# Attention and gated feed-forward on one core: another transfer model, another set of rules for the order

## Chip, cores and metric

The kernel runs on one core of one Trainium2 chip. The metric is the device time in microseconds (us); lower is better. Each engine of the core (TensorE or PE, ScalarE or ACT, VectorE or DVE, GpSimd or POOL, SyncE or SP) has its own instruction stream; semaphores tie them together. SP here issues all transfers (DMAs).

## The reference

One sequence of S = 2048 rows of width D = 512, in bf16. The result is the input plus an attention block plus a gated feed-forward block, both fed by the same layer norm. There are 32 heads of 16 elements each; the feed-forward is 1792 wide.

```python
def _A_ref(x, wqkv, wo):
    qkv = (x @ wqkv).reshape(B, S, 3, H, Dh).transpose(2, 0, 3, 1, 4)
    q, k, v = qkv[0], qkv[1], qkv[2]
    scores = jnp.einsum("bhqd,bhkd->bhqk", q, k) * (Dh ** -0.5)
    p = _softmax(scores, axis=-1)
    o = jnp.einsum("bhqk,bhkd->bhqd", p, v)
    return o.transpose(0, 2, 1, 3).reshape(B, S, D) @ wo

def _B_ref(x, w1, w3, w2):
    h = _silu(x @ w1) * (x @ w3)
    return h @ w2

x = A_x
xn = _layernorm(x, axis=-1)
return x + _A_ref(xn, A_wqkv, A_wo) + _B_ref(xn, B_w1, B_w3, B_w2)
```

## The kernel before

**Work.** Heads go four at a time (8 groups g), queries 512 at a time (4 chunks qc). A query unit u is one group with 256 queries; the first three units and the last sixteen are smaller, 128 queries for the most part. For each unit the scores are computed twice.

In pass one (p1) a row-tiled matmul of 32 contraction rows (L1371) writes scores of 128 queries against 512 keys into a bank of PSUM; two neighbouring banks hold 1024 scores, and VectorE takes the row maximum of each half (`tensor_reduce`, L1416). 998 of these run. In some places a "split" replaces part of this: ScalarE makes RB (L1484), and VectorE finishes it (L1409). The maxima of a unit are joined on GpSimd (L1538 to L1552, for the last units on VectorE at L1575), spread into Z (L1520, L1522), and brought as two extra rows into Q: by a DMA transpose (L1568) and two DMAs (L1564), or for the first and last units by matmuls (tile `AQ`). A DMA (L1502) also copies Q of each head into a block-diagonal tile BD.

In pass two (p2) the scores come again, transposed, keys on partitions, with the maximum already subtracted by the extra rows. The matmuls are row-tiled (L1653), or "wide" with BD as the moving operand over the full array. ScalarE takes the exponential of one bank of 512 (L1678), or of two neighbouring banks in one instruction of 1024 (L1709), a **pair**. Then PV (tile `PV`, L777) multiplies by V with a column of ones; ScalarE moves the result to U (L1773). The normaliser follows as a chain with one unit in it at a time: DMA Lc from U (L1794), reciprocal on GpSimd (L1798), DMA to DRAM rd (L1803), broadcast DMA back into R (L1807), multiply on GpSimd (L1834), and for odd groups four small DMAs (L1830).

The feed-forward (tiles `G`, `U`, with ScalarE at L1089, L1093, L1083 and GpSimd at L1060, L1064) and the output projection (`OUT`, at the end `OUTA` and `OUTB`) are fitted in between. Their weights come by DMA at L727 and L729, the residual at L1117, stores go at L1148.

**Order.** No instruction's place is written by hand. While the program is built, a planner keeps a clock for each engine and a ready time for each buffer, and gives out the next instruction to the engine that could start first. `pick_pe`, `pick_act`, `pick_dve`, `pick_pool` and `pick_sp` propose, each by cost figures in the code. For a transfer, `later_dma` notes `occ` (how long SP is taken by issuing it), `lat` (from issue to landing) and `busy` (the share of the transfer engines). The result is five static instruction lists. On the chip each runs strictly in its order, and only semaphores decide the times: a wrong cost figure gives waits, not wrong data.

**Rules.** The proposals depend on some 45 constants (`RULES`), among them `A_LEAD` (how long ahead a row maximum's scores are wanted), `PAIR_WAIT` (how long ScalarE may be held for a pair), `HEAT_FILL`, `HEAT_WIDE`, `HEAT_FORCE`. The planner cuts its progress into 256 segments of 12 steps; `TUNE` names for each segment one of the `SETS`, which override some constants.

**Heat.** `_heat` gives each matmul a weight, and `heat(t)` sums weight times duration over the 3.413 us before t. Below `HEAT_FILL` a filler matmul, whose result nobody reads (`fill_cand`), may be put in where it fits; below `HEAT_WIDE` pass two prefers its wide form; below `HEAT_FORCE` a matmul that works on columns is put in even if it doesn't fit ahead of the next score.

**Pairs.** `pick_act` looks at the first few waiting exponentials; if two lie in neighbouring banks and the second is ready no more than `PAIR_WAIT` later, they become one instruction.

Of the kernel before, what the change touches and what calls it, by code (L numbers as in the profile page):

```python
# [268 lines left out]
def _build(nc, A_x, A_wqkv, A_wo, B_w1, B_w3, B_w2, out):  # L269
# [48 lines left out]
    BD_END = 4  # L318
    NORM = "dddppppp"
# [12 lines left out]
        dict(PAIR_WAIT=0.15, RELAX=0.05),  # L332
        dict(P2_FRAG=0.0, URG_WAIT=0.05, A_LEAD=0.82, PAIR_WAIT=0.15),
        dict(P1_SLIP=0.15, P1_TRI=1, P2_MID=3, P1_EARLY=0.15),
        dict(P2_MID=3, PV_LEFT=2, TOL=0.15, PAIR_DEPTH=3),
        dict(LAZY_MAX=6.0, A_LEAD=0.55),
        dict(WIDE_LEAD=0.3, TOL=0.1),
        dict(A_LEAD=0.82, P2_MID=5, HEAT_WIDE=0.47),
        dict(TOL=0.0, PV_LEFT=2, A_LEAD=0.55, AGAIN=3),
        dict(RELAX=0.1, PACE=12000),  # L340
        dict(PAIR_TEN=0, TEN_MID=1),
        dict(A_LEAD=0.69, HEAT_FILL=0.82, URG_WAIT=0.15),
        dict(OUT_GATE=14, TOL=0.1),
        dict(PAIR_DEPTH=5, HEAT_TILE=0.5, PAIR_WAIT=0.15),
        dict(W_WAIT=0.1, RELAX=0.2),
        dict(HEAT_FORCE=0.5, PAIR_TEN=2),
        dict(P1_SLIP=0.15, BD_NEAR=0.5, RELAX=0.05, HEAT_TILE=0.5),
        dict(MIN_PIECE=3, LAZY_GAP=0.05, PAIR_TEN=0, HEAT_WIDE=0.57),
        dict(HEAT_FILL=0.82, PACE=3000, A_LEAD=0.82),
        dict(HEAT_FILL=0.82, PACE=12000, P1_SLIP=0.15, FILL_SLIP=0.1),  # L350
        dict(ROW_LEAD=0.55, WIDE_LEAD=0.45, BD_NEAR=0.1),
        dict(HEAT_FILL=0.7, LAZY_GAP=0.3, FILL_SLIP=0.1),
        dict(URG_WAIT=0.05, P1_EARLY=0.3, HEAT_WIDE=0.57, LAZY_MAX=1.0),
        dict(ROW_LEAD=0.62, FILL_SLIP=0.1),
        dict(BD_NEAR=0.5),
# [12 lines left out]
        dict(BD_NEAR=0.1),
        dict(P2_NEAR=0.1, HEAT_P1=0.35, A_LEAD=0.88, HEAT_WIDE=0.57),
        dict(HEAT_FILL=0.82),  # L370
        dict(FILL_SLIP=0.1, W_WAIT=0.1, P2_NEAR=0.02, WIDE_LEAD=1.0),
        dict(WIDE_LEAD=0.7, BD_NEAR=0.8, COUPLE=0.08, HEAT_P1=0.65),
        dict(A_LEAD=0.88, HEAT_WIDE=0.34, URG_WAIT=0.05),
        dict(WIDE_LEAD=0.7, BD_NEAR=0.1, W_WAIT=0.2),
        dict(A_LEAD=0.82),
        dict(PACE=12000, PAIR_WAIT=0.05, P2_NEAR=0.4, COUPLE=0.18),
        dict(HEAT_TILE=0.65, P2_MID=3, WIDE_LEAD=0.2, HEAT_FILL=0.82),
        dict(WIDE_LEAD=0.7, P2_NEAR=0.1, FILL_SLIP=0.0, A_LEAD=0.82),
        dict(PAIR_WAIT=0.1, HEAT_FILL=0.82),
        dict(TOL=0.05, BD_NEAR=0.1, AGAIN=2, PAIR_WAIT=0.0),  # L380
        dict(BD_NEAR=0.2),
        dict(HEAT_FILL=0.55, W_WAIT=0.2, HEAT_P1=0.65, MIN_PIECE=3),
        dict(RELAX=0.1, PAIR_DEPTH=2, FILL_SLIP=0.0, BD_NEAR=0.1),
        dict(A_LEAD=0.55, LAZY_MAX=1.0, COUPLE=0.25, P1_TRI=1),
        dict(HEAT_TILE=0.7, A_LEAD=0.72),
        dict(BD_NEAR=0.5, W_WAIT=0.2, PAIR_DEPTH=4, P1_SAME=0.2),
        dict(FILL_SLIP=0.2, WIDE_LEAD=0.3),
        dict(MIN_PIECE=2, TOL=0.05, WIDE_LEAD=0.7, W_WAIT=0.1),
        dict(A_LEAD=0.6, HEAT_FORCE=0.41, WIDE_LEAD=0.7),
        dict(A_LEAD=0.69, WIDE_LEAD=1.0),  # L390
        dict(HEAT_P1=0.55, BD_NEAR=0.5),
        dict(LAZY_GAP=0.3, A_LEAD=0.69),
        dict(A_LEAD=0.69, P1_EARLY=0.15, COUPLE=0.25),
        dict(PV_LEFT=3, MIN_PIECE=2, RELAX=0.05, P1_SLIP=0.15),
        dict(W_WAIT=0.1, ROW_LEAD=0.4),
        dict(COUPLE=0.04, OUT_GATE=20, HEAT_FILL=0.45, P1_SAME=0.05),
        dict(RELAX=0.05),
        dict(P1_EARLY=0.3, P1_SAME=0.05, HEAT_FILL=0.7, PAIR_TEN=0),
        dict(HEAT_FILL=0.45),
        dict(HEAT_P1=0.35, HEAT_FILL=0.45, PAIR_TEN=0),  # L400
        dict(PAIR_TEN=2, RELAX=0.05),
        dict(ROW_LEAD=0.55),
        dict(PACE=12000, MIN_PIECE=4, HEAT_P1=0.65, AGAIN=4),
        dict(PV_LEFT=8, HEAT_WIDE=0.57, TOL=0.05, LAZY_GAP=0.02),
        dict(HEAT_FILL=1.2, P2_FRAG=0.0, RELAX=0.2),
        dict(HEAT_FILL=0.5, WIDE_LEAD=1.0, HEAT_TILE=0.5, TOL=0.03),
        dict(ROW_LEAD=0.55, PV_LEFT=2, HEAT_FILL=0.7, PAIR_WAIT=0.0),
        dict(COUPLE=0.04, URG_WAIT=0.15, HEAT_WIDE=0.57),
        dict(HEAT_TILE=0.53),
        dict(A_LEAD=0.88, HEAT_WIDE=0.57, TOL=0.0),  # L410
        dict(LAZY_MAX=1.0, HEAT_FORCE=0.36, P2_MID=3),
        dict(PAIR_DEPTH=1, LAZY_MAX=6.0, A_LEAD=0.69, TRI_WAIT=0.1),
        dict(HEAT_FILL=0.55),
        dict(HEAT_FILL=0.5, BD_NEAR=0.5),
        dict(A_LEAD=0.69, HEAT_FORCE=0.42),
        dict(TRI_WAIT=0.3, P2_NEAR=0.0, P2_MID=2, BD_NEAR=0.8),
        dict(A_LEAD=0.6),
        dict(HEAT_P1=0.0, ROW_LEAD=0.43, AGAIN=4, LAZY_GAP=0.02),
        dict(P1_SAME=0.2, ROW_LEAD=0.43, P2_NEAR=0.4),
        dict(URG_WAIT=0.05, PAIR_WAIT=0.1, HEAT_WIDE=0.47),  # L420
        dict(LAZY_MAX=6.0, ROW_LEAD=0.62, P1_SLIP=-0.15),
        dict(MIN_PIECE=2, HEAT_FILL=0.4, RELAX=0.1, OUT_GATE=32),
        dict(COUPLE=0.18, P2_MID=2, HEAT_FILL=0.82),
        dict(P1_TRI=1, PACE=3000, P2_NEAR=0.2, PAIR_TEN=2),
        dict(HEAT_P1=0.0, HEAT_FILL=0.82),
        dict(PAIR_TEN=2, HEAT_FILL=1.2),
        dict(P1_SAME=-0.1, PACE=12000, HEAT_P1=0.55, TRI_WAIT=0.3),
        dict(A_LEAD=0.72),
        dict(HEAT_P1=0.49, PAIR_DEPTH=2, A_LEAD=0.69, HEAT_TILE=0.65),
        dict(HEAT_P1=0.61),  # L430
        dict(P1_SAME=0.2, A_LEAD=0.88),
        dict(ROW_LEAD=0.35, P2_FRAG=0.2, PAIR_DEPTH=5),
        dict(MIN_PIECE=2, ROW_LEAD=0.5),
        dict(PAIR_WAIT=0.05, W_WAIT=0.2),
        dict(BD_NEAR=0.2, TOL=0.03, WIDE_LEAD=0.3, P1_SLIP=0.15),
        dict(ROW_LEAD=0.4, P2_NEAR=0.2),
        dict(LAZY_MAX=6.0, HEAT_P1=0.65),
        dict(TOL=0.05),
        dict(ROW_LEAD=0.5),
# [24 lines left out]
    )
# [14 lines left out]
    class K:  # L479
# [15 lines left out]
        P1_SLIP=0.0,  # L495
# [55 lines left out]
    with ctx:  # L551
# [1793 lines left out]
```

## Time and profile before

| | us |
|---|---|
| median of 3 runs | 1198.87 |
| lowest, highest | 1196.85, 1200.25 |
| the profiled execution, its own time | 1193.87 |
| its span in the profile | 1192.1 |
| busy: PE, VectorE, ScalarE, GpSimd | 1123.6, 1166.7, 1166.2, 452.0 |
| first row maximum starts, last one ends | 14.25, 1168.4 |
| exponentials: of 512, of 1024 (pairs) | 1728, 160 |

The span runs from the first instruction to the last. Instructions of ScalarE overlap: one of 512 lasts 715 ns by its own record, and the next starts before it ends. So prices of ScalarE are read from start to start, and a busy time of 98% may hold small gaps. In a group of instructions the columns are: line, engine, operation, output<-input, count, then busy us and mean ns, then the idle time ahead of them and what ended it. Windows give for each stretch the busy us of each engine, the number of instructions that start in it, and the TensorE clock that was granted (1.00 is full speed).

### The profile page before, as it was taken

The numbers are of one execution on the slowest core, as the hardware profiler recorded it, in microseconds if no ns is written. First come the engines' busy times: TensorE is split into PE (matmuls) and PEld (weight loads), VectorE is DVE, ScalarE is ACT, GpSimd is POOL, SyncE is SP. The second block draws the span as 40 slices with busy tenths as digits, with TensorE's granted clock in tenths as the row PEclk, the third lists the DMA queues.
The fourth block names the chain that finished last, engine by engine and source line by source line (L and its number), as shares of the span: only waits on it lengthen the run. The fifth ranks groups of instructions, "written<-read, shape, count | busy, mean of one in ns | idle before, by whom it ended". The sixth has DMA issues, their size and how long they took to land.

```text
span 1192.1 us, 36419 instructions
## 1 busy us (share of the span) xinstructions
PE 1123.6 (94%) x15037; PEld 529.2 (44%) x15171; DVE 1166.7 (98%) x1091; ACT 1166.2 (98%) x2245; POOL 452.0 (38%) x888
## 2 busy tenths in 40 slices
PE   8989999999999999999999999999999999998998
PEld 4433434443444444334444444434434444354654
DVE  8999999999999999999999999999999999998995
ACT  8899999999999999999999999999999999998997
POOL 7145453444424254334432234533442214621220
PEclk9999999999999999999999999999999999999999
DMA  8233322211111121111111122111110112000010
GB/s 247 73 77 80 90 55 54 56 28 41 38 43 29 41 59 38 41 40 28 46 30 24 38 56 61 43 33 36 38 30 24 41 48 49 19 23 21 15 22 22
DMA packets 141641, 55.96 MB, mean 47 GB/s; under 512 B 103968, under 2 KB 141476, under 8 KB 141476
## 3 DMA queue, kind: packets, MB, share of 16 engines
q1 hardware_dynamic: 141476, 53.63, 17.4%
q8 instruction: 120, 1.97, 0.7%
q14 instruction: 45, 0.37, 0.1%
HBM read 38.93 MB, written 6.74 MB: 38 GB/s over the span
## 4 chain that ended last, share of the span: by engine, by line
ACT 67%; DVE 14%; PE 12%; DMA 3%; issue 2%; SPq 1%; POOL 1%
ACT PT L1678 51%; DVE part L1416 14%; ACT PT L1709 8%; PE ps L773 5%; PE ps L777 3%; PE ps L1371 2%; PE ps L1653 2%; ACT zg L1089 2%; ACT th L1083 1%; ACT ub L1093 1%; ACT U L1773 1%; DMA rd<-Rc 1%; ACT RB L1484 1%; DMA R<-rd 1%; ACT kq L961 1%
## 5 line engine op out<-in xcount | busy, mean ns | idle before, releaser
L1416 DVE TENSOR_REDUCE part<-ps 128x2 f32<-128x1024 f32 x998 | 1133.2, 1216 | 6.9 <-PE ps L1653 3.5
L1678 ACT ACTIVATE PT<-ps 128x512 bf16<-128x512 f32 x1728 | 918.8, 715 | 6.5 <-PE ps L1653 2.4
L1653 PE MATMUL ps<-QT,KT 32*128 32x256 bf16 (+1 forms) x3420 | 457.0, 258 | 8.8 <-DMA QT<-Zs 1.1
L1371 PE MATMUL ps<-KT,QT 32*128 32x512 bf16 x2158 | 431.5, 384 | 8.3 <-DVE part L1416 4.2
L1653 PEld LDWEIGHTS ps<-QT,KT 32*128 32x128 bf16 x3420 | 161.5, 93 | 167.1 <-ACT PT L1678 70.2
L777 PE MATMUL ps<-PT,Vaug 128*17 128x256 bf16 (+1 forms) x4672 | 197.9, 261 | 3.5 <-ACT PT L1678 0.7
L1709 ACT ACTIVATE PT<-ps 128x1024 bf16<-128x1024 f32 x160 | 177.0, 1123 | 0.3 <-PE ps L1653 0.2
L1371 PEld LDWEIGHTS ps<-KT,QT 32*128 32x128 bf16 x2158 | 107.9, 91 | 145.0 <-DVE part L1416 63.0
L773 PE MATMUL ps<-xnT,w 128*128 128x512 bf16 (+3 forms) x612 | 153.3, 309 | 12.4 <-ACT PT L1678 3.4
L1798 POOL TENSOR_TENSOR Rc<-Lc,mone 128x8 f32<-128x8 f32 (+1 forms) x69 | 104.8, 1519 | 117.3 <-DMA Lc<-U 116.9
L773 PE MATMUL ps<-BD,KT 128*128 128x256 bf16 (+1 forms) x790 | 135.1, 265 | 3.1 <-ACT PT L1709 0.9
L777 PEld LDWEIGHTS ps<-PT,Vaug 128*17 128x17 bf16 x4672 | 92.8, 90 | 75.6 <-issue 54.1
L773 PE MATMUL ps<-xnT,ident 128*128 128x512 bf16 (+3 forms) x314 | 80.5, 323 | 10.0 <-DVE part L1416 3.1
L773 PEld LDWEIGHTS ps<-xnT,w 128*128 128x128 bf16 x661 | 51.2, 97 | 82.6 <-issue 44.8
L777 PE MATMUL ps<-BD,KT 128*32 128x256 bf16 (+1 forms) x1848 | 83.5, 265 | 2.9 <-DMA BD<-QT 2.6
L773 PE MATMUL ps<-w,hT 128*128 128x128 bf16 (+3 forms) x335 | 81.7, 301 | 3.6 <-ACT U L1773 2.7
L1545 POOL TENSOR_TENSOR mx<-part 128x16 f32<-128x16 f32 (+1 forms) x60 | 14.2, 237 | 180.7 <-DVE part L1416 180.5
L1834 POOL TENSOR_TENSOR wk_on<-U,R 128x256 bf16<-128x256 f32 (+1 forms) x36 | 22.9, 635 | 139.6 <-DMA R<-rd 139.6
L773 PEld LDWEIGHTS ps<-BD,KT 128*128 128x128 bf16 x790 | 60.9, 98 | 32.5 <-ACT PT L1678 7.2
L1064 POOL TENSOR_TENSOR hT<-a,t 128x512 bf16<-128x512 f32 x56 | 71.0, 1268 | 2.4
L1834 POOL TENSOR_TENSOR on_b<-U,R 128x256 bf16<-128x256 f32 (+1 forms) x33 | 23.5, 711 | 126.1 <-DMA R<-rd 126.1
L1060 POOL TENSOR_SCALAR t<-th 128x512 f32<-128x512 bf16 x56 | 34.8, 621 | 84.4 <-ACT th L1083 82.8
(114 smaller groups left out, 753.8 us busy)
## 6 DMA issues: line engine op xcount, KB each, us to landing
w<-in_B_w_dram SPq DMA_DIRECT2D x112, 128.0 KB
R<-rd SPq DMA_DIRECT2D x55, 128.0 KB
QT<-qd SPq DMA_DIRECT2D x31, 128.0 KB
KT<-kd SPq DMA_DIRECT2D x28, 128.0 KB
BD<-QT SPq DMA_DIRECT2D x220, 10.5 KB
xr<-in_A_x_dram SPq DMA_DIRECT2D x16, 128.0 KB
out_dram<-osb SPq DMA_DIRECT2D x16, 128.0 KB
qd<-kq SPq DMA_DIRECT2D x15, 128.0 KB
```

The source lines that it names most:

```text
L773: return e.matmul(bank(bk)[:, c0 + a:c0 + b], make_lhsT(0, 128), rhs_ap(0)[:, a:b], start=start, stop=stop, **kw)
L777: ins = e.matmul(bank(bk)[32 * i:32 * i + m, c0 + a:c0 + b], make_lhsT(i), rhs if (a, b) == (0, ncols) else rhs[:, a:b], start=start, stop ...
L1060: q.append(_Item(lambda e: e.tensor_scalar(t1[:, :], th[:, ss, :], 1.0, 1.0, ALU.mult, ALU.add), [("th", ss)], [("t1",)], 0.62, 0.72))
L1064: q.append(_Item(lambda e: e.tensor_tensor(hT[:, hslot(idx), :], a32[:, :], t1[:, :], ALU.mult), [("a32",), ("t1",)], [("hT", hslot(idx))] ...
L1089: return [_Item(lambda e: e.activation(zg[:, ss, :], bank(bk), ACTF.Identity, scale=0.5), [("ps", bk)], [("zg", ss)], _c_act(512), cb=zg_d ...
L1371: ins = e.matmul(bank(held[i]), QT[32 * j:32 * j + 32, qs, q * 128:(q + 1) * 128], KT[32 * j:32 * j + 32, g, c_ * 512:(c_ + 1) * 512], sta ...
L1416: redq.append(_Item(lambda e: e.tensor_reduce(dst, banks, AX.X, ALU.max), writes, [("part", par, i_) for i_ in ix[:m]], _c_dve(512 * m), c ...
L1653: ins = e.matmul(bank(b)[:, i * nq:(i + 1) * nq], KT[32 * j:32 * j + 32, g, (k0 + i) * 128:(k0 + i + 1) * 128], QT[32 * j:32 * j + 32, qs, ...
L1678: expq.append(_Item(lambda e: e.activation(PT[:, sl, :], bank(b), ACTF.Exp, scale=SCALE), [("ps", b)], [("PT", sl)], _c_act(512), cb=cb, e ...
L1709: return _Item(lambda e: e.activation(PT[:, s0:s1 + 1:s1 - s0, :], two_banks(b0, b1), ACTF.Exp, scale=SCALE), [("ps", b0), ("ps", b1)], [( ...
L1798: poolq["nrm"].append(_Item(lambda e: e.tensor_tensor(Rc[:, pp, 0:nl], Lc[:, pp, 0:nl], mone[:, 0:nl], ALU.pow), [("Lc", pp), ("mone",)], ...
L1834: poolq["nrm"].append(_Item(lambda e: e.tensor_tensor(onorm[ob][:, oslot(ob, g), q0:q0 + nq], U[:, us, 0:nq], R[:, pp, 0:nq], ALU.mult), [ ...
```

## The change

1. Transfers get figures of their own. `later_dma` takes `occ` for each kind instead of 0.62 for nearly all, and `slow`, a later landing that counts once pass one has passed step 24 (`STEADY`).

| transfer (line before) | occ before, after | lat before, after step 24 |
|---|---|---|
| feed-forward weights (L727, L729) | 0.62, 0.5 | 2.5, 3.6 |
| K and Q to DRAM (L932) | 0.62, 0.7 | 2.75, 3.3 |
| K back (L949), Q back (L954) | 0.62, 0.43 | 2.2, 3.3 and 3.0 |
| residual (L1117) | 0.62, 0.5 | 2.3, 4.0 |
| store (L1148) | 0.62, 0.45 | 2.3, 2.5 |
| BD (L1502) | 0.62, 0.77 | 2.1, 2.4 |
| extra rows (L1564) | 0.62, 0.58 | 2.0, 2.3 |
| transpose (L1568) | 1.25, 1.25 | 3.0, 3.4 |
| Lc (L1794) | 0.62, 0.66 | 2.0, 2.35 |
| rd (L1803) | 0.62, 0.43 | 1.7, 2.1 |
| R (L1807) | 0.62, 0.66 | 3.7, 3.9 |
| odd groups' moves (L1830) | 0.62, 0.62 | 2.2, 3.0 |

2. Each transfer has a rank; where `SP_RANK` is 1, of transfers that could start at the same time the one of the lower rank goes first.

3. PV's weight in `_heat` rises from 0.52 to 0.85; the default constants of heat change.

4. `SETS` (134 before, 161 after) and `TUNE` are replaced; 22 segments used the defaults before, 19 after.

What is computed doesn't change, nor do the constants that cut it into units and splits.

```diff
-    return 0.52 if name.startswith("PV") else 0.25 if name.startswith("tr") else 0.97
+    return 0.85 if name.startswith("PV") else 0.25 if name.startswith("tr") else 0.97
...
+    BD_SLOW = 2.4
+    STEADY = 24
...
     SETS = (
         dict(),
         dict(A_LEAD=0.88, RELAX=0.1),
-        dict(PAIR_WAIT=0.15, RELAX=0.05),
-        dict(P2_FRAG=0.0, URG_WAIT=0.05, A_LEAD=0.82, PAIR_WAIT=0.15),
...
+        dict(RELAX=0.1, PACE=12000),
+        dict(PAIR_TEN=0, PV_LEFT=4, P1_SLIP=0.15, HEAT_FILL=0.5),
...
     TUNE = (
-        1, 2, 3, 4, 5, 6, 7, 8, 9, 10, 11, 0, 12, 13, 0, 14, 15, 16, 17, 18, 19, 20, 21, 22,
...
+        1, 2, 3, 4, 5, 6, 7, 8, 9, 10, 11, 12, 13, 14, 15, 16, 17, 18, 19, 20, 0, 21, 22, 23,
...
+        SP_RANK=0,
...
-        HEAT_FILL=.42,
-        HEAT_WIDE=0.,
-        HEAT_FORCE=0,
+        HEAT_FILL=.65,
+        HEAT_WIDE=0.37,
+        HEAT_FORCE=.38,
...
-        def later_dma(fn, reads, writes, lat=2.3, cb=None, pred=None, occ=0.62, busy=0.1):
-            spq.append(_Item(fn, reads, writes, occ, lat, cb, pred, busy=busy))
+        steady = [False]
+
+        def later_dma(fn, reads, writes, lat=2.3, cb=None, pred=None, occ=0.62, busy=0.1, slow=None, rank=3):
+            spq.append(_Item(fn, reads, writes, occ, slow if steady[0] and slow is not None else lat, cb, pred, busy=busy, exp=rank))
...
                 later_dma(lambda e: e.dma_start(rd_[pp][0:4 * nq].rearrange("(p n) -> p n", n=nl), Rc[:, pp, 0:nl]),
-                          [("Rc", pp)], [("rd", pp)], lat=1.7, cb=n4)
+                          [("Rc", pp)], [("rd", pp)], lat=1.7, occ=0.43, slow=2.1, rank=1, cb=n4)
...
-                    if b is None or s < b[0] - 1e-6:
+                    if b is None or s < b[0] - 1e-6 or (K.SP_RANK and s < b[0] + 1e-6 and it.exp < spq[b[1]].exp):
...
+            steady[0] = p1_n[0] >= STEADY
```

More of the change, by code (lines that the diff above doesn't have):

```diff
@@ new lines, in _build @@
+        dict(FILL_SLIP=0.0, SP_RANK=1),
+        dict(P1_SLIP=-0.15, WIDE_LEAD=1.0),
+        dict(PAIR_WAIT=0.0, BD_NEAR=0.1),
+        dict(A_LEAD=0.88, P1_SAME=0.2, FILL_SLIP=0.1, AGAIN=2),
+        dict(TOL=0.05, BD_NEAR=0.1, AGAIN=2, PAIR_WAIT=0.0),
+        dict(FILL_SLIP=0.2),
+        dict(A_LEAD=0.82, P2_MID=5, HEAT_WIDE=0.47),
+        dict(OUT_GATE=32),
+        dict(P1_SAME=0.05, TRI_WAIT=0.1, HEAT_TILE=0.7, BD_NEAR=0.8),
+        dict(LAZY_MAX=1.0, P1_TRI=1, HEAT_FILL=0.42, ROW_LEAD=0.55),
@@ new lines, in _build @@
+        dict(LAZY_MAX=6.0, P2_FRAG=0.2, A_LEAD=0.6),
+        dict(URG_WAIT=0.05, PAIR_WAIT=0.1, HEAT_WIDE=0.47),
+        dict(PV_LEFT=10, ROW_LEAD=0.62, AGAIN=1, PACE=3000),
+        dict(LAZY_MAX=6.0, A_LEAD=0.55),
+        dict(MIN_PIECE=4, TRI_WAIT=0.1),
+        dict(COUPLE=0.18, A_LEAD=0.55),
+        dict(TOL=0.03, WIDE_LEAD=0.7, P2_NEAR=0.4),
+        dict(HEAT_FILL=0.82, PACE=3000, A_LEAD=0.82),
+        dict(PV_LEFT=6, ROW_LEAD=0.5, HEAT_P1=0.61),
+        dict(P2_MID=5, P1_EARLY=0.3, SP_RANK=1),
@@ L1147, in store @@
         def store(tg):
-            later_dma(lambda e: e.dma_start(out_v[:, tg, :], osb[:, tg % 4, :]), [("osb", tg % 4)], [("out", tg)], busy=0.4,
+            later_dma(lambda e: e.dma_start(out_v[:, tg, :], osb[:, tg % 4, :]), [("osb", tg % 4)], [("out", tg)], busy=0.4, occ=0.45, slow=2.5,
                       cb=lambda op: done.add(("ST", tg)))
```

280 lines of the change are left out of this document (144 added, 136 removed), and 20 rows, old and new, of the table TUNE.

## The prediction, on record before the run

> **What bounds the kernel now.** I read the page's totals first, then a table of stretches, then the chain of waits, and last the timelines at the places that these point to.
>
> ```profile
> span 1192.1 us, 36419 instructions
> PE 1123.6 (94%) x15037; PEld 529.2 (44%) x15171; DVE 1166.7 (98%) x1091; ACT 1166.2 (98%) x2245; POOL 452.0 (38%) x888
> ...
> L1416 DVE TENSOR_REDUCE part<-ps 128x2 f32<-128x1024 f32 x998 | 1133.2, 1216 | 6.9 <-PE ps L1653 3.5
> L1678 ACT ACTIVATE PT<-ps 128x512 bf16<-128x512 f32 x1728 | 918.8, 715 | 6.5 <-PE ps L1653 2.4
> ...
> L1709 ACT ACTIVATE PT<-ps 128x1024 bf16<-128x1024 f32 x160 | 177.0, 1123 | 0.3 <-PE ps L1653 0.2
> ```
>
> Two engines are at 98% and a third at 94%. Averages don't say where the rest went, so the span is cut at the first row maximum (14.2), at the two places where the waits gather, and at the last row maximum (1168.4). Columns: stretch, its length, then busy us (and starts) of PE, PEld, DVE, ACT, POOL, the granted clock, DMA share, GB/s.
>
> ```profile
> 0.00:14.20 14.20, 10.82 (x93) 7.77 (x93) 10.47 (x28) 9.62 (x22) 6.94 (x25) 1.00 0.91 285
> 14.20:150.00 135.80, 125.92 (x1460) 55.52 (x1475) 133.15 (x120) 126.92 (x237) 62.28 (x114) 1.00 0.35 95
> 150.00:1050.00 900.00, 859.30 (x10701) 387.11 (x10796) 899.90 (x809) 899.08 (x1737) 355.84 (x688) 1.00 0.16 40
> 1050.00:1100.00 50.00, 43.94 (x1024) 27.19 (x1024) 46.54 (x45) 46.48 (x93) 10.70 (x29) 0.97 0.09 21
> 1100.00:1168.40 68.40, 65.12 (x1403) 41.84 (x1413) 67.68 (x68) 67.69 (x139) 15.76 (x32) 1.00 0.09 19
> 1168.40:1192.10 23.70, 18.48 (x368) 9.79 (x371) 8.92 (x26) 16.41 (x24) 0.46 (x1) 0.98 0.07 24
> ```
>
> This is the argument in one table. From 14.2 to 1168.4 the row maxima on VectorE set the pace, and VectorE is idle in that time for 135.80-133.15 = 2.65, 900.00-899.90 = 0.10, 50.00-46.54 = 3.46 and 68.40-67.68 = 0.72 us: **6.9 us** in all. For three quarters of the kernel there is nothing to regain. Ahead of it lie 14.2 us of loads and layer norm, behind it 23.7 us of tail, in which ScalarE still works 16.41 us. So an order that leaves the work alone can win from three places: the stall before 150, the one between 1050 and 1100, and the tail.
>
> **Where the stalls come from.** The chain of waits (start, us, what) through the late one, and the table around it:
>
> ```profile
> 1063.94 3.08 DMA rd<-Rc
> 1067.05 3.35 DMA R<-rd
> ...
> 1070.47 0.19 POOL wk_on L1834
> ...
> 1072.89 0.58 SPq L1830
> ...
> 1077.20 2.08 DMA rd<-Rc
> ...
> 1088.60 2.40 DMA rd<-Rc
> 1091.03 2.64 DMA R<-rd
> ...
> 1093.74 0.17 POOL wk_on L1834
> ...
> 1095.43 0.23 POOL Z L1522
> ```
>
> ```profile
> 1092.00:1094.00 2.00, 1.64 (x49) 0.98 (x44) 2.00 (x4) 1.45 (x3) 0.26 (x1) 1.00 0.18 43
> 1094.00:1096.00 2.00, 0.30 (x4) 0.30 (x5) 1.13 (x1) 1.19 (x2) 1.56 (x4) 0.92 0.01 3
> 1096.00:1098.00 2.00, 1.67 (x17) 0.89 (x16) 0.90 (x1) 1.71 (x4) 0.00 (x0) 0.50 0.03 6
> 1098.00:1100.00 2.00, 1.94 (x27) 0.92 (x25) 1.49 (x3) 1.35 (x4) 0.00 (x0) 0.72 0.05 4
> ```
>
> The broadcast of the reciprocals (rd, then R) lands; only then does GpSimd run the normalising multiply (L1834), and queued behind that, in order, the Z items that the next query unit's scores need. PE stood with 0.30 us of work in 1094 to 1096, and the granted clock was 0.50 just after. One late landing therefore costs twice, by the wait and by half speed behind it.
>
> The code assumed 1.7 us for rd and 3.7 for R, 5.4 together. The trace shows from one start to GpSimd's multiply 1070.47-1063.94 = 6.53 and 1093.74-1088.60 = 5.14. The new figures are 2.1 and 3.9, 6.0 together: nearer to the long one, safe against the short one.
>
> The early stall, from the chain and from VectorE's timeline:
>
> ```profile
> 120.46 0.48 SPq L727
> ...
> 121.06 0.81 SPq L1502
> 121.91 2.01 DMA BD<-QT
> ```
>
> ```profile
> 125.08 2.49 DVE L1416 TENSOR_REDUCE part<-ps 128x2 f32<-128x1024 f32 x2 [1.53 <-PE ps L1371]
> ```
>
> Here it is the order of SP's queue: a weight load (0.48 to issue) and a BD copy (0.81), both costed at 0.62 before. The change says 0.5 and 0.77. Those two figures at least are right by this trace.
>
> **The change part by part.**
> *Transfer times.* They alter no instruction, only the order in which all five queues are written. What they can return is the idle time of VectorE in the two stretches: at most 2.65 + 3.46 = 6.1 us, at least less than nothing, since another order has late landings of its own. The late stall has one identified cause that the new figures address; I take back two thirds of it, 2.3. The early one has several; I take half, 1.3. Against it I set 0.9 of new waits, a quarter of the late stall's price, for an order whose landings nobody has seen. What is late next, when these waits are gone, is the row maxima themselves. Together **-2.7 us**.
>
> *Queues passed.* The ranks (augmented rows, normaliser, BD, the rest) act only where SP_RANK is 1, in 5 of 256 segments, so the queue's order elsewhere follows from the times alone. Moving a load later on SP holds every transfer behind it; its cover is the prefetch of two slots for w13 and xr, and when that is gone the price is the early stall's 1.53 us.
>
> *Paired exponentials.* ScalarE's timeline gives both prices by start to start:
>
> ```profile
> 299.32 8.13 ACT L1678 ACTIVATE PT<-ps 128x512 bf16<-128x512 f32 x16
> 307.10 0.63 ACT L1773 ACTIVATE U<-ps 128x256 f32<-128x256 f32 x1
> ...
> 1172.04 2.93 ACT L1709 ACTIVATE PT<-ps 128x1024 bf16<-128x1024 f32 x3
> 1174.75 0.71 ACT L1678 ACTIVATE PT<-ps 128x512 bf16<-128x512 f32 x1
> 1175.22 1.15 ACT L1709 ACTIVATE PT<-ps 128x1024 bf16<-128x1024 f32 x1
> ```
>
> Sixteen singles take 307.10-299.32 = 7.78, 0.486 each; three pairs 2.71, 0.903 each; the lone single there 0.47. A pair saves between 2x0.47-0.903 = 0.04 and 2x0.486-0.903 = 0.07 us; I take 0.05. (The Trainium skill, ScalarE: Activation LUTs, section What ACT_TABLE_LOAD costs, gives 186 ns + 0.833 ns per element with an overlap of about 93 ns, so about 0.09 us saved by a pair; the rows show little more than half of that, and stand. By that rule 60 pairs would be worth 5.6 us.)
>
> How many are added isn't in the diff: the segments that raise PAIR_WAIT are 10 before and 10 after, so they follow from when neighbouring banks are ready. Saved time on ScalarE counts only as far as its lag at 1168.4 shrinks. In the tail the last unit alone needs 16 tiles, 8 pairs, 8x0.903 = 7.2 us; ScalarE works 16.41, so **9.2 us are lag**. Bounds: 0 (none added, or all spent while it waits for VectorE anyway) and 9.2 (180 or more added). I take 60 that reach the tail, 60x0.05 = **-3.0 us**; what is late after that is the last row maximum itself, then PV, projection and store, which stay.
>
> *Heat.* PV's assumed weight goes from 0.52 to 0.85, the default threshold for filler from 0.42 to 0.65, and matmuls may now be forced where the computed heat is below 0.38 (0 before). Filler hides in PE's idle time, 900.00-859.30 = 40.7 us in the long stretch; while it does, it costs nothing. It may save a half-speed window, already counted in the 3.46.
>
> *Sum.* 1192.1-2.7-3.0 = 1186.4 for the span. The profiled execution's own time was 1193.87, 1.8 above its span, and the median of the three runs, 1198.87, lies 5.0 above that. Kept so: 1186.4+1.8+5.0 = **1193.2 us**, 0.5% faster. That the plain runs are longer than the profiled one I can't explain by a row; if they contain more half-speed windows, the added filler gains there besides, which I don't count.
>
> **The rivals.**
> *One for one.* The new order removes these stalls and has others of the same size, and the added pairs are spent waiting for VectorE, or there are none. For it: VectorE's pace is fixed and 0.10 us is lost in 900, and ScalarE is busy 16.41 us in the tail whatever was paired before. Against: the known stall is one cause. Time: 1198.87 less 0 to 3.6, about 1197.5; the change does not do what it says in effect.
>
> *Forced matmuls fill PE.* Place: 150 to 1050. The price of one from PE's timeline, and the fillers of before:
>
> ```profile
> 1088.12 0.72 PE L773 MATMUL ps<-xnT,ident 128*128 128x512 bf16 x3
> ```
>
> ```profile
> L773 PE MATMUL ps<-xnT,ident 128*128 128x512 bf16 (+3 forms) x314 | 80.5, 323 | 10.0 <-DVE part L1416 3.1
> ```
>
> One of 512 columns takes 0.72/3 = 0.24 us. The idle 40.7 us hold 40.7/0.24 = 170 more. From there on each delays a score by its length: 200 more give 200x0.24-40.7 = +7.3 us and a time near 1206. For it: the threshold rises in nearly all segments, and forcing sets aside whether the piece fits before the next score. Against: unforced filler goes only where it fits, and PV's higher weight lifts the computed heat, which holds filler back.
>
> *Pairs hold banks longer* would also be slower, but two stretches speak against it, pairs in the first two rows, row maxima in the others:
>
> ```profile
> 450.00:500.00 50.00, 15.62 (x15) 1.00 0.14 34
> 650.00:700.00 50.00, 1.76 (x2) 1.00 0.15 39
> ```
>
> ```profile
> 450.00:500.00 50.00, 48.84 (x44) 1.00 0.14 34
> 650.00:700.00 50.00, 48.95 (x44) 1.00 0.15 39
> ```
>
> With 15 pairs or with 2, VectorE starts 44 row maxima in 50 us. I give it no time of its own.
>
> **How the numbers follow.** The measurement tells about 0.3% from no change, 3.6 us: 1195.3 to 1202.5 is the same. Forecast (both gains, in whole or in part): 0.56, between 1198.87-6.1-9.2 = 1183.6 and 1195.3, most likely 1193.2. One for one: 0.27. Forced matmuls, or a new late landing at the old one's price: 0.17, from 1202.5 to 1206 and beyond. The range leaves out the last third of the bounds below, where both stalls and nearly all lag would have to go, and the worse half of the slow case: 1186 to 1203.
>
> **What would show it.** Right: VectorE's idle time between first and last row maximum below 5 us, above all in 1050 to 1100; no clock of 0.50 there; well over 200 pairs; ScalarE's busy time after the last row maximum near 13 us. Wrong: row maxima that end no sooner than 1166; the same 16 us of tail with more pairs; a PE over 890 us in the long stretch with VectorE idle beside it; a wait of GpSimd's multiply for R followed by an idle PE at a new place.

## The result, and the profile after

Five runs of each kernel, one after the other: **1190.92 us** after (1186.81 to 1191.9) against 1197.25 before (1195.53 to 1200.25), ratio 0.9934, interval [0.9909, 0.9958]: 0.66% faster. A second set, with the kernels unchanged, gave 1188.24 (6 runs) against 1199.77 (29 runs), ratio 0.9922 [0.9897, 0.9947]. A few executions that ran far longer, among them the one that was profiled for the last experiment, are left out here and below.

The page of the changed kernel: its totals, the row maxima, the two groups of exponentials and the filler. Lines have moved (L1448 is L1416 of before, L1710 is L1678, L1741 is L1709):

```profile
span 1190.2 us, 36200 instructions
...
PE 1144.1 (96%) x15064; PEld 513.5 (43%) x15064; DVE 1166.3 (98%) x1091; ACT 1162.1 (98%) x2161; POOL 452.2 (38%) x888
...
L1448 DVE TENSOR_REDUCE part<-ps 128x2 f32<-128x1024 f32 x998 | 1132.6, 1209 | 5.0 <-PE ps L1685 4.1
L1710 ACT ACTIVATE PT<-ps 128x512 bf16<-128x512 f32 x1560 | 832.7, 666 | 8.2 <-PE ps L1685 3.0
...
L1741 ACT ACTIVATE PT<-ps 128x1024 bf16<-128x1024 f32 x244 | 263.1, 1109 | 0.0
...
L805 PE MATMUL ps<-xnT,ident 128*128 128x512 bf16 (+3 forms) x572 | 157.3, 334 | 18.9 <-ACT PT L1741 8.5
```

VectorE does the same 998 row maxima. Pairs went from 160 to 244. The filler (xnT with ident) went from 345 to 572 instructions of the full form: the 314 and 80.5 us of the first profile of before are short of some matmul records (its page has 15037 matmuls beside 15171 weight loads). The second profile of the kernel before has them all:

```profile
L773 PE MATMUL ps<-xnT,ident 128*128 128x512 bf16 (+3 forms) x345 | 90.7, 333 | 7.2 <-DVE part L1416 3.0
```

So the filler grew from 90.7 to 157.3 us. The table of stretches, cut at this kernel's own first and last row maximum:

```profile
14.00:150.00 136.00, 132.57 (x1451) 56.75 (x1451) 135.91 (x123) 130.16 (x248) 64.05 (x115) 1.00 0.35 92
150.00:1050.00 900.00, 869.31 (x10673) 372.59 (x10669) 896.88 (x806) 892.65 (x1651) 351.57 (x682) 1.00 0.16 41
1050.00:1100.00 50.00, 46.25 (x1102) 27.00 (x1098) 49.16 (x47) 49.22 (x92) 13.84 (x35) 1.00 0.10 21
1100.00:1166.70 66.70, 64.42 (x1389) 38.29 (x1386) 65.80 (x69) 64.42 (x133) 15.20 (x32) 1.00 0.09 18
1166.70:1190.20 23.50, 19.96 (x371) 10.41 (x368) 8.06 (x22) 15.91 (x22) 0.71 (x2) 1.00 0.09 28
```

VectorE's idle time is now 0.09, 3.12, 0.84 and 0.90 us, 4.95 in all (6.9 before). The early stall is gone and the one after 1050 is small (both again in a second profile, below), but the long stretch, which had lost 0.10, loses 3.12. The tail is 23.5 us, as good as unchanged, and ScalarE works 15.91 us in it (16.41 before). Where the 3.12 went, from the chain of waits and from a table of the place:

```profile
760.73 0.79 SPq L1534
...
761.57 3.55 DMA BD<-QT
...
765.16 0.93 PE ps L809 x12
```

```profile
762.00:764.00 2.00, 0.97 (x14) 0.34 (x14) 2.00 (x2) 1.81 (x4) 1.83 (x3) 1.00 0.09 23
764.00:766.00 2.00, 0.84 (x12) 0.23 (x12) 0.18 (x1) 0.29 (x1) 1.92 (x3) 0.83 0.29 72
766.00:768.00 2.00, 2.00 (x16) 0.50 (x13) 1.32 (x2) 1.16 (x3) 1.01 (x1) 0.50 0.05 12
```

A BD copy took 3.55 us (the new assumption is 2.4), a wide matmul at the head of PE's queue waited for it, and the clock was at half just behind: the pattern of before at another place.

### The profile page after: what moved, and what is told of

It reads as the page before. It is cut to its first block, busy times and chain, and to the rows that moved or that the text cites. A ratio compares the mean times of both kernels' runs of the same rounds, so it can differ in the third digit from the quotient of the medians.

```text
span 1190.2 us, 36200 instructions
## 1 busy us (share of the span) xinstructions
PE 1144.1 (96%) x15064; PEld 513.5 (43%) x15064; DVE 1166.3 (98%) x1091; ACT 1162.1 (98%) x2161; POOL 452.2 (38%) x888
## 3 DMA queue, kind: packets, MB, share of 16 engines
q8 instruction: 119, 1.95, 0.7%
## 4 chain that ended last, share of the span: by engine, by line
ACT 48%; DVE 30%; PE 18%; issue 2%; DMA 1%; POOL 1%; SPq 0%; POOLq 0%; DVEq 0%
ACT PT L1710 33%; DVE part L1448 29%; ACT PT L1741 9%; PE ps L805 7%; PE ps L809 5%; PE ps L1685 4%; PE ps L1403 3%; ACT zg L1121 1%; ACT th L1115 1%; ACT ub L1125 1%; ACT U L1805 1%; ACT RB L1516 1%; DMA BD<-QT 1%; PE ps L2067 1%; ACT kq L993 1%
## 5 line engine op out<-in xcount | busy, mean ns | idle before, releaser
L1448 DVE TENSOR_REDUCE part<-ps 128x2 f32<-128x1024 f32 x998 | 1132.6, 1209 | 5.0 <-PE ps L1685 4.1
L1710 ACT ACTIVATE PT<-ps 128x512 bf16<-128x512 f32 x1560 | 832.7, 666 | 8.2 <-PE ps L1685 3.0
L1403 PE MATMUL ps<-KT,QT 32*128 32x512 bf16 x2096 | 423.9, 384 | 2.0 <-DVE part L1448 1.4
L1741 ACT ACTIVATE PT<-ps 128x1024 bf16<-128x1024 f32 x244 | 263.1, 1109 | 0.0
L1685 PEld LDWEIGHTS ps<-QT,KT 32*128 32x128 bf16 x3780 | 168.5, 92 | 174.0 <-issue 72.4
L809 PE MATMUL ps<-PT,Vaug 128*17 128x256 bf16 (+1 forms) x4672 | 190.4, 261 | 3.2 <-ACT PT L1741 0.7
L805 PE MATMUL ps<-xnT,ident 128*128 128x512 bf16 (+3 forms) x572 | 157.3, 334 | 18.9 <-ACT PT L1741 8.5
L1403 PEld LDWEIGHTS ps<-KT,QT 32*128 32x128 bf16 x2096 | 104.9, 91 | 133.4 <-issue 66.2
L1830 POOL TENSOR_TENSOR Rc<-Lc,mone 128x8 f32<-128x8 f32 (+1 forms) x69 | 104.8, 1518 | 109.2 <-DMA Lc<-U 109.1
L805 PE MATMUL ps<-BD,KT 128*128 128x256 bf16 (+1 forms) x562 | 100.6, 267 | 0.5 <-DMA BD<-QT 0.3
L805 PEld LDWEIGHTS ps<-xnT,ident 128*128 128x128 bf16 x572 | 45.6, 97 | 98.7 <-ACT PT L1710 36.3
L805 PE MATMUL ps<-w,hT 128*128 128x512 bf16 (+3 forms) x326 | 78.0, 316 | 0.0
L1094 POOL TENSOR_TENSOR a<-zg,ub 128x512 f32<-128x512 bf16 x56 | 64.6, 1153 | 2.5 <-ACT ub L1125 2.5
```

The source lines that it names most:

```text
L805: return e.matmul(bank(bk)[:, c0 + a:c0 + b], make_lhsT(0, 128), rhs_ap(0)[:, a:b], start=start, stop=stop, **kw)
L809: ins = e.matmul(bank(bk)[32 * i:32 * i + m, c0 + a:c0 + b], make_lhsT(i), rhs if (a, b) == (0, ncols) else rhs[:, a:b], start=start, stop ...
L1094: q.append(_Item(lambda e: e.tensor_tensor(a32[:, :], zg[:, ss, :], ub[:, ss, :], ALU.mult), [("zg", ss), ("ub", ss)], [("a32",)], 1.1, 1.25))
L1403: ins = e.matmul(bank(held[i]), QT[32 * j:32 * j + 32, qs, q * 128:(q + 1) * 128], KT[32 * j:32 * j + 32, g, c_ * 512:(c_ + 1) * 512], sta ...
L1448: redq.append(_Item(lambda e: e.tensor_reduce(dst, banks, AX.X, ALU.max), writes, [("part", par, i_) for i_ in ix[:m]], _c_dve(512 * m), c ...
L1685: ins = e.matmul(bank(b)[:, i * nq:(i + 1) * nq], KT[32 * j:32 * j + 32, g, (k0 + i) * 128:(k0 + i + 1) * 128], QT[32 * j:32 * j + 32, qs, ...
```

## The experiments

**The two kernels again**, unchanged.

> The kernel before, unchanged, for the span and the granted clock of each single run and for a second profile of the same order. If the stall near 1093 us belongs to the order (transfers queued badly), the second profile has it again within a few us of that place, with VectorE losing about 3 us there. If it was one late landing by chance, it is gone and the loss lies elsewhere. If half-speed windows make the spread between runs, runs with clock 1.000 are the shortest and each 0.001 of clock below that (about two windows' third) goes with 2 to 4 us.

> The changed kernel, unchanged, for the same two questions. In its first profile VectorE lost 2.6 us at 763 us behind a BD copy that took 3.55 us to land. If that late landing is chance, the second profile doesn't have it there; if it belongs to the order, it does. Two of its runs had clock 1.000 and spans of 1185.0 and 1186.6, three had 0.998 or 0.999 and 1189.2 to 1190.2: if the windows explain the spread, new runs fall on the same two levels.

Measured: 1198.89 and 1188.24. The second profile of the kernel before has a span of 1204.4, 12.3 longer than the first, at a mean clock of 0.987. Some of its stalls are those of the first profile and some are not. A late execution shifts all times, so a place is better named by the row maximum that waits, counted from the first. The early stall stands ahead of the 96th in both profiles (1.53 us, now 2.37), the late one begins ahead of the 941st in both (0.87, now 1.95) with further waits among the next eleven, and a third stands ahead of the 991st (0.68, now 2.58):

```profile
126.59 108.15 DVE L1416 TENSOR_REDUCE part<-ps 128x2 f32<-128x1024 f32 x95 [2.37 <-PE ps L1371]
...
1091.94 1.22 DVE L1416 TENSOR_REDUCE part<-ps 128x2 f32<-128x1024 f32 x1 [1.95 <-PE ps L1371]
...
1155.89 1.23 DVE L1416 TENSOR_REDUCE part<-ps 128x2 f32<-128x1024 f32 x1 [2.58 <-PE ps L1653]
```

These belong to the order, as the first branch of the expectation said. Between 14.2 and 150 VectorE is idle for 135.80-131.88 = 3.92 us here, against 2.65 in the first profile and 0.09 and 0.07 in the two of the changed kernel; between 1050 and 1100 for 4.36 us, against 3.46, and 0.84 and 1.53 in the changed kernel, whose late stall stands ahead of the 952nd both times. The stall at 435 us is not in the first profile at all; chain and table:

```profile
433.51 1.82 DMA BD<-QT
```

```profile
430.00:432.00 2.00, 2.00 (x44) 0.91 (x40) 2.00 (x2) 1.80 (x5) 1.87 (x3) 1.00 0.05 12
432.00:434.00 2.00, 1.75 (x23) 0.61 (x22) 1.90 (x3) 2.00 (x5) 1.43 (x2) 1.00 0.21 56
434.00:436.00 2.00, 0.54 (x4) 0.44 (x4) 0.63 (x1) 0.18 (x1) 0.00 (x0) 0.70 0.10 30
436.00:438.00 2.00, 2.00 (x12) 0.67 (x9) 1.05 (x1) 1.39 (x3) 0.00 (x0) 0.50 0.32 73
438.00:440.00 2.00, 2.00 (x14) 0.55 (x13) 1.40 (x2) 1.87 (x4) 1.77 (x2) 0.50 0.61 135
440.00:442.00 2.00, 1.93 (x15) 0.72 (x11) 1.26 (x2) 1.13 (x3) 1.41 (x8) 0.59 0.27 56
```

In the second profile of the changed kernel the stall at 763 is gone, by the expectation a late landing by chance. VectorE works 1147.34 of 1149.50 us between its first and last row maximum, and the tail is again 23.6. For comparison the first line is the first profile of before, whose mean clock is the same 0.998:

```profile
14.20:1168.40 1154.20, 1094.29 (x14582) 511.65 (x14707) 1147.27 (x1038) 1140.18 (x2202) 444.57 (x863) 1.00 0.18 44
```

```profile
13.70:1163.20 1149.50, 1112.38 (x14601) 495.18 (x14601) 1147.34 (x1042) 1136.40 (x2120) 446.58 (x864) 1.00 0.18 45
1163.20:1186.80 23.60, 19.98 (x371) 10.42 (x368) 8.08 (x22) 15.93 (x22) 0.62 (x2) 0.99 0.09 28
```

At the same clock, then, VectorE is busy for the same time (1147.27 and 1147.34 us), and the difference of 5.4 us in the span is nearly all idle time of VectorE, 6.93 against 2.16.

Each run's mean clock puts a number on the half speed. A straight line through the 40 runs of the kernel before in this set gives 1192.7 us at clock 1.000 and 0.98 us more for each 0.001 less (correlation -0.81); their median clock is 0.993. Through the 11 runs of the changed kernel it gives 1188.2 and 1.1 us, and six of them stand at 1.000. Half speed comes in windows: the clock's shortfall from 1094 to 1100 in the prediction's table is 2x(0.08+0.50+0.28) = 1.72 us, 3.4 us at half speed, and the one of 434 to 442 above is 2x(0.30+0.50+0.50+0.41) = 3.42, 6.8 us or twice as long. The code's own constant is 3.413. One such window takes 0.5x3.413/1190 = 0.0014 from the mean clock, so it goes with about 1.4 us, the wait that brought it included, and the kernel before has 0.007/0.0014 = 5 of them in a median run; the first profile, with 0.998, was a lucky one. **So of the gain of 11.5 us in this set 4.5 are there at full clock, and about 7 go with windows that no longer occur.** The 4.5 is the less certain: the same line through the runs of the kernel before in the two later sets ends at 1191.6 and 1191.0, which would leave 3 us.

**Pairs.** Same order, each pair written as two exponentials in its place; then only 84 of the 244.

```diff
-            return _Item(lambda e: e.activation(PT[:, s0:s1 + 1:s1 - s0, :], two_banks(b0, b1), ACTF.Exp,
-                                                scale=SCALE),
+            def two(e):
+                e.activation(PT[:, s0, :], bank(b0), ACTF.Exp, scale=SCALE)
+                return e.activation(PT[:, s1, :], bank(b1), ACTF.Exp, scale=SCALE)
+            return _Item(two,
```

> The changed kernel's order, with each of the 244 pairs written as two exponentials of 512 in the same place, so that only ScalarE's price changes, by 244 x 0.05 = 12 us. Theory one (pairs count as far as they shrink ScalarE's lag at the last row maximum): the end moves by 3 to 9 us, and the lag after the last row maximum grows by about as much. Rival (VectorE's pace and the stalls decide, pairs are slack): less than 2 us.

Measured: 1202.2, 14.0 above the changed kernel; clock 1.000. That is 14.0/244 = 0.057 each, all of it and more than I gave. But it is not where I put it, and neither theory one nor its rival (under 2 us) described it. Row maxima's stretch and tail of this kernel:

```profile
14.10:1176.50 1162.40, 1118.40 (x14600) 494.07 (x14601) 1157.06 (x1041) 1149.38 (x2351) 446.64 (x864) 1.00 0.18 44
1176.50:1200.80 24.30, 20.71 (x371) 10.81 (x369) 8.21 (x23) 16.80 (x35) 0.46 (x1) 1.00 0.09 26
```

The tail grew by 0.7 only; the last row maximum ended 13.3 later. And VectorE is "busy" 1157.06 instead of 1147.34 us with the same row maxima. Of the 14.0 us, 9.7 are in this busy time, 3.2 in idle time (5.34 instead of 2.16), and the rest at the two ends. This is how ScalarE's price shows here: a row maximum lasts 1.21 us by its record but the next starts 1.13 after it, so a start can slip by some 0.08 without any idle time appearing. VectorE's timelines of the split and of the changed kernel show it:

```profile
299.50 31.27 DVE L1448 TENSOR_REDUCE part<-ps 128x2 f32<-128x1024 f32 x27
```

```profile
299.28 31.75 DVE L1448 TENSOR_REDUCE part<-ps 128x2 f32<-128x1024 f32 x28
```

27 row maxima in 31.27 us against 28 in 31.75, both rows without a gap. With the last one's 1.21 us taken off, that is (31.27-1.21)/26 = 1.156 us from start to start against (31.75-1.21)/27 = 1.131. The mean over all 998 is less, 9.7/998 = 0.010 us each. What PE waited for ahead of the scores of the row maxima (L1403; us in total, times) points the same way, first the split, then the changed kernel:

```profile
  DVE part L1448: 26.1, 71
  ACT PT L1743: 6.7, 23
```

```profile
  DVE part L1448: 50.3, 159
  ACT PT L1741: 4.0, 14
```

PE waited less for banks that VectorE gives back and somewhat more for those of the exponentials, which fits row maxima whose scores come later.

> The changed kernel's order, with 84 of its 244 pairs, spread evenly, written as two exponentials each, so that 160 pairs are left, as many as before. If all of ScalarE's price reaches the end, as with all 244 (13.9 us over the unsplit one, 0.057 each), the time is 84 x 0.057 = 4.8 us above the changed kernel, at the same clock of 0.999 to 1.000. Rival (only the pairs near the tail count): under 1.5 us.

Measured: 1192.82, 4.6 above the changed kernel (by the ratios to the kernel before of each set, 0.9956 [0.9933, 0.998] and 0.9922, 4.1); at full clock 1192.5 by its line. So the new order with 160 pairs is at full clock about as long as the old one with its 160 (1192.7, or 1191.6 by the line through this set). But 84 pairs are not shown to be what the new order gained over the old. VectorE is busy 1151.11 us here between its first and last row maximum, and 1147.27 in the old order, which has as many pairs, where the planner put them.

**SP's queue before.** In the old order one rd store is issued ahead of the moves before it.

```diff
+        spl = P.ops["sp"]
+        at = next(i for i, op in enumerate(spl) if getattr(op.fn, "tag", None) == ("rd", 57))
+        to = at
+        for i in range(at - 1, max(at - 9, 0), -1):
+            if getattr(spl[i].fn, "tag", ("",))[0] == "mv":
+                to = i
+        spl.insert(to, spl.pop(at))
```

> The kernel before with one edit of SP's list: the store of the reciprocals (rd) of unit 57 goes ahead of the four small moves and two row copies that stand before it near 1073 us; nothing else changes. Theory one (the late stall comes from the order of SP's queue and the chain of the normaliser): rd issues about 3.5 us sooner, the normalising multiply follows, the stall of VectorE near 1093 us shrinks from 3 to under 1 us, and the time falls by 2 to 4 us. Rival (late landings are chance, or the chain recovers anyway): no change within 1 us.

Measured: 1200.01, ratio 1.0011 [0.9983, 1.0039], clock 0.9915. The gain that theory one forecast did not come. But the test is weak, as SP's timeline of its profile shows:

```profile
1076.68 0.57 SPq L1804 DMA_DIRECT2D rd<-Rc  x1
1077.31 2.47 SPq L1833 DMA_DIRECT2D wk_on<-wk_on  x4
1079.82 1.17 SPq L1564 DMA_DIRECT2D QT<-Zs  x2
1081.03 1.26 SPq L1568 DMA_TRANSPOSE Zs<-Z  x1
1082.34 0.58 SPq L1809 DMA_DIRECT2D R<-rd  x1
```

The reciprocal of this unit starts at 1074.49 here and at 1071.15 in the first profile. So rd issues 2.19 us after it instead of 6.05, as meant. But the moves and copies that it passed now stand ahead of R, which issues 7.85 us after the reciprocal instead of 8.15, and the multiply follows 10.57 us after it (1085.06) instead of 10.95 (1082.10). The chain became 0.4 us shorter, not 3.5. What VectorE lost:

```profile
1050.00:1100.00 50.00, 46.91 (x1070) 27.87 (x1064) 48.80 (x47) 48.37 (x97) 12.80 (x37) 0.98 0.10 21
1100.00:1168.40 68.40, 64.86 (x1206) 39.43 (x1207) 61.67 (x60) 62.46 (x126) 14.23 (x29) 0.89 0.08 17
```

VectorE loses 50.00-48.80 = 1.2 us there instead of 3.46, and 68.40-61.67 = 6.7 right behind, at a clock of 0.89; there a broadcast R took 4.93 us, against 2.64 in the first profile. Whether the normaliser's chain is the cause of the late stall stays open.

**The filler.** The changed kernel's order with each filler cut to two columns.

```diff
-                P.pe(col_groups(bk, lambda i, z=32: ident[:, 32 * i:32 * i + z], lambda i: xnT[:, 0, 0:128 * k], 128 * k,
+                P.pe(col_groups(bk, lambda i, z=32: ident[:, 32 * i:32 * i + z], lambda i: xnT[:, 0, 0:2], 2,
```

> The changed kernel's order with every filler matmul cut to 2 columns, in the same places; PE does some 100 us less work. Theory two (the filler holds the clock, and that is half of the gain): the granted clock falls below 0.98 and the time rises by 1 us for each 0.001, 15 us or more. Rival (filler only takes PE's time; the clock is held by the real work): clock unchanged, time the same or up to 3 us shorter.

Measured: 1273.56, 85 us longer than the changed kernel, clock 0.87. The scores of pass two, first here, then in the changed kernel:

```profile
L1685 PE MATMUL ps<-QT,KT 32*128 32x256 bf16 (+1 forms) x3780 | 528.8, 286 | 9.7 <-ACT PT L1741 2.4
```

```profile
L1685 PE MATMUL ps<-QT,KT 32*128 32x256 bf16 (+1 forms) x3780 | 460.8, 258 | 5.2 <-ACT PT L1741 1.7
```

The same scores take 286 ns instead of 258. Theory two holds: in this order work that nobody reads holds the clock. Each 0.001 costs 85/130 = 0.65 us here, less than the 1 us forecast.

**One part at a time.** Here each edit makes the planner write another order, so pairs and filler change too. `b_newheat` and `b_newtimes` take one part of the change into the kernel before; `a_oldheat`, `a_oldtimes` and `a_oldrules` put one part of the changed kernel back.

```diff
 b_newheat, from the kernel before:
+    return 0.85 if name.startswith("PV") else 0.25 if name.startswith("tr") else 0.97
+        HEAT_FILL=.65, HEAT_WIDE=0.37, HEAT_FORCE=.38,
 a_oldheat, from the changed kernel:
+    return 0.52 if name.startswith("PV") else 0.25 if name.startswith("tr") else 0.97
+        HEAT_FILL=.42, HEAT_WIDE=0., HEAT_FORCE=0,
 a_oldtimes, from the changed kernel:
+            spq.append(_Item(fn, reads, writes, 1.25 if occ == 1.25 else 0.62, lat, cb, pred, busy=busy, exp=rank))
 a_oldrules: SETS and TUNE of before; b_newtimes: these and the old heat
```

> The kernel before with the new weight of PV and the three new heat constants, and nothing else; its order has more filler, and 139 pairs. Theory two: clock 0.998 to 1.000 instead of 0.993, time 1192.7 (the kernel before at full clock) plus 1.2 for 21 pairs fewer, about 1194, 5 us below before, and a spread of runs of 5 us instead of 12. Rival (the gain is in the transfer times): no change, or slower, since these rules were searched for other constants.

> The changed kernel with the old weight of PV and the three old heat constants; its order has less than half of the filler, and 226 pairs. Theory two: clock 0.98 to 0.993, time 1188.2 plus 1.0 for 18 pairs fewer plus 7 or more for the clock, 1196 or more, spread of runs over 8 us. Rival (transfer times): it keeps at least two thirds of the gain, under 1193.

> The kernel before with the new transfer times alone: old rules, old heat. Its order has 132 pairs, 28 fewer than before, worth 28 x 0.055 = +1.5 us. Theory three (half-speed windows start behind transfers that land later than the order assumed, a BD copy at the head of PE's queue or the normaliser's broadcast ahead of Z on GpSimd): fewer windows, clock 0.996 or more instead of 0.993, time 1192 + 1.5 + at most 4 = 1194 to 1198. Rival (the heat rules and their search hold the clock, whatever the transfers): clock 0.993 or less and 1200 or more.

> The changed kernel with the old transfer times: new rules, new heat, 141 pairs (103 fewer, worth +5.7 us). Theory three: windows come back, clock 0.994 or less, time 1188 + 5.7 + 6 = 1200 or more. Rival (heat rules hold the clock): clock 0.998 or more and a time near 1194.

> The changed kernel with the old sets of rules: new transfer times and new heat constants, nothing searched for them; 105 pairs (139 fewer, +7.6 us) and as much filler as the changed kernel has. If times and heat together hold the clock: 0.998 or more, time about 1196. If it takes the search over the rules to hold it: clock 0.994 or less, 1202 or more.

The runs of this table come from three sets, in which the kernel before stood at 1199.77, 1199.58 and 1196.76 us; the ratio is to the kernel before of the same set.

| kernel | transfer times | heat | rules | filler | pairs | median clock | us | ratio to before |
|---|---|---|---|---|---|---|---|---|
| before | old | old | old | 345 | 160 | 0.993 | 1199.77 | 1 |
| b_newheat | old | new | old | 576 | 139 | 0.993 | 1201.08 | 1.0022 [0.9995, 1.005] |
| a_oldtimes | old | new | new | 533 | 141 | 0.994 | 1203.4 | 1.0067 [1.004, 1.0094] |
| b_newtimes | new | old | old | 293 | 132 | 0.975 | 1216.08 | 1.0168 [1.012, 1.0216] |
| a_oldheat | new | old | new | 210 | 226 | 0.921 | 1265.81 | 1.057 [1.0528, 1.0612] |
| a_oldrules | new | new | old | 551 | 105 | 0.9975 | 1200.72 | 1.0022 [1.0, 1.0044] |
| after | new | new | new | 572 | 244 | 1.000 | 1188.24 | 0.9922 [0.9897, 0.9947] |

(Filler: weight loads of the full form in the profile; some profiles are short of matmul records.) None of these five wins anything over the kernel before, and two lose much; the new rules alone were not run. My expectations of b_newheat (0.998 and 1194) and b_newtimes (0.996 and 1194 to 1198) failed, each the way its rival said. Of a_oldheat the direction held, but it lost far more than forecast. a_oldtimes came as theory three said (0.994 or less, 1200 or more). a_oldrules fell between its two branches, its clock near the first and its time near the second.

Read in pairs: with much filler, the old times stand at 0.993 and 0.994, the new at 0.9975 and 1.000. With little filler the clock falls, and the fewer the fillers the further: 345, 293 and 210 go with 0.993, 0.975 and 0.921. So new times and much filler together go with the highest clocks. Whether the new times without the new heat are worse in themselves, or only by their 52 fewer fillers, these orders don't separate. The rules give pairs and a tail. The tails of the two orders whose rules were not searched for their constants are these, ScalarE's work in them being the fourth busy time:

```profile
1164.50:1196.90 32.40, 27.62 (x584) 15.21 (x582) 10.32 (x29) 22.73 (x35) 1.91 (x3) 1.00 0.07 21
```

```profile
1165.90:1200.00 34.10, 26.90 (x625) 14.39 (x623) 9.06 (x27) 28.66 (x42) 2.88 (x4) 0.94 0.08 22
```

a_oldrules and a_oldtimes end their row maxima as soon as the changed kernel, 1164.5 and 1165.9, and lose it in a tail of 32.4 and 34.1 us. ScalarE works 22.73 and 28.66 us in these tails, 6.8 and 12.7 more than in the changed kernel's 15.93, with 139 and 103 pairs fewer, priced at 7.6 and 5.7. So in orders that the planner makes anew, ScalarE's arrears can gather behind the last row maximum, as the prediction supposed; these orders differ in more than pairs, so this is not shown to be the pairs' doing.

**BD copies later.** The changed kernel's order, with six waits for an event already past ahead of each BD copy on SP.

```diff
+            if getattr(op.fn, "bd", False):
+                k, v = op.deps[0].token
+                for _ in range(6):
+                    handle.wait_ge(dma_sems[k[1]] if isinstance(k, tuple) else sems[k], v)
             ins = op.fn(handle)
```

> The changed kernel's order, with SP made to wait six times more for an event already past ahead of each BD copy, so that the four copies of a unit issue and land later, the last of them by some 0.4 to 0.8 us; nothing else changes. Theory three: PE stands more often at a wide matmul, windows come back (clock 0.997 or less) and the time rises by 3 to 10 us. Rival (late copies are harmless, chance starts the windows): clock 0.999 to 1.000, time within 1.5 us of the changed kernel.

Measured: 1196.7, ratio to before 0.9986 [0.996, 1.0012], clock 0.996 to 0.999. In its trace four copies in a row take SP 3.6 us instead of 3.0, so the last is 0.6 us later; every transfer behind them on SP is later too. By the ratios (0.9986 against 0.9922) some 8 us are lost against the changed kernel. Windows come back, worth 1 to 4 us by their clock; the rest is perhaps the waits themselves, which isn't shown. The time is as theory three forecast, and the clock is close to it (median 0.9975, forecast 0.997 or less): later transfers bring windows and cost time. Whether it is the BD copies or what stands behind them, and at which places, no trace shows.

## Why the prediction was right, and which step failed

The time (1193.2) and the range held, and so did the likeliest case, "both gains, in whole or in part". That it came so near is in part luck: the forecast of -5.7 us met -6.3 in the first set, but -11.5 in the second, and of its terms one was too small, one came by another way, and one was left out.

The signs were mixed. Of the four for "right", three came in the first profile: VectorE's idle time below 5 us (4.95 and 2.16), no clock of 0.50 in 1050 to 1100 (in the first profile; the second has a mean of 0.97 there, so one window), and over 200 pairs (244). ScalarE's 13 us after the last row maximum did not: it was 15.91. Of those for "wrong", two came: the same 16 us of tail with more pairs, and, in the first profile alone, row maxima that end no sooner than 1166 (1166.7, then 1163.2).

*The stalls* were put at -2.7. In both profiles of each kernel the early stall went (2.65 and 3.92 us before, 0.09 and 0.07 after; I took half), and the late one shrank (3.46 and 4.36 to 0.84 and 1.53; I took 2.3). So this term was right in kind and too small. The new waits cost 3.02 in the long stretch of one profile, against my 0.9, and nothing of that kind in the other. Transfer times were credited with the stalls by themselves, and that failed: alone they make the kernel 1.7% slower (ratio 1.0168 [1.012, 1.0216]).

*The pairs* were put at -3.0: 60 of them at 0.05, and this through ScalarE's lag at the last row maximum. The size was low, 84 pairs at 0.055 being 4.6. **The mechanism failed.** "ScalarE works 16.41, so 9.2 us are lag" led me to a shorter tail; the tail stayed at 23.5. In the new order a pair that is split makes PE wait longer for ScalarE, and VectorE's row maxima start later all along: 1.156 instead of 1.131 us each in the stretch shown, where all pairs were split. I had read "899.90 of 900" as proof that nothing was to be had there, but overlapping records hide such slips. The count of 44 row maxima in 50 us with 15 pairs or with 2 could not show them either: 44x0.025 is 1.1 us, one row maximum at most. For the old order itself no experiment shows what pairs would bring, and VectorE's busy time there was no longer than in the new one.

*Heat* was the term with no price: filler "costs nothing", a saved window was "already counted in the 3.46". The windows were the largest part: about 7 us of the second set's difference go with 5 windows in the old kernel's median run. With the filler cut the new order loses 85 us, so the filler is needed for it; but the new heat constants alone do not bring it (b_newheat stands at 0.993, as before). The text saw that plain runs are longer than the profiled one, named more windows as the cause that it could not show, and counted nothing. Carrying over the 5.0 us between profile and median was wrong for that reason: 1190.92 is 1.0 below the changed kernel's profiled 1191.9.

*The rival* of forced matmuls did not come: PE works 869.31 of 900 us in the long stretch, under the 890 that I had named, with 1.7 times the filler. The room of 40.7 us was read too large, since the first profile lacks about 95 matmul records there (10701 beside 10796 weight loads); the second profile of before, with all of them, has 874.32 us, which leaves 25.7. PE's load did not grow with the filler; wide matmuls with BD became fewer, 1882 instead of 2638 in the second profiles.

Open: which of the heat constants does it, how much of the gain is due to each part when they only win together, and whether the normaliser's chain or the BD copies cause the late stall.

## What to carry to other kernels

Compare several runs' clocks before a profile is trusted as the typical run: here one number per run, the granted clock, went with two thirds of the variance over 16 us of spread. Name a stall by the instruction that waits, not by the time: three stalls of the old order came back at the same row maxima. An engine whose records overlap can lose time at 100% busy, so check its pace from start to start. And a cost model's truer figures can make an order worse, here by 1.7%, until the rest is searched with them.

## What was not expected of the hardware

One window of half speed goes with some 1.4 us of time, the wait that brought it included. It doesn't take an idle PE: at 434 to 436 us of the second profile of before the clock averaged 0.70, so half speed began near 434.8, and of the 3.42 us ahead of that PE was busy 2.35 (431.40 to 434.82). At 230.02 us of the same profile half speed began after 3.42 us in which PE was busy 3.22, from 226.8 to 228.7 on row-tiled matmuls alone. The Trainium skill (TensorE: Matmul & The Clock Gate, Part 1) has the clock halved after at least one idle window of about 3.4 us; the length agrees with the 3.4 us worked out above, the idleness doesn't, by PE's busy records, in which the ends of matmuls are modelled. In the changed kernel's order, matmuls whose result nobody reads, 157.3 us of them in the full form, are worth 85 us. The same kind of BD copy landed in 1.82 us in one place and in 3.55 in another.
